# Row normalisation moved to GpSimd, separate slots for the shared passes, and a first q projection in two column groups, in a fused attention and gated MLP kernel

## The chip, the cores and the metric

The kernel runs on one core of a Trainium2 chip. The core has five engines that run side by side, each through its own queue in order: TensorE (PE, matrix products into PSUM; its weight loads are listed as PEld), VectorE (DVE), ScalarE (ACT), GpSimd (POOL) and SyncE (SP, which issues the DMAs). They wait for each other through semaphores. The metric is the device time of one execution in microseconds.

## The reference

The input x has 2048 rows of 512. It is normalised by rows, and two branches read the result: an attention with 32 heads of 16 columns, and a gated MLP with 1792 hidden columns. Their sum is added to x.

```python
S, D, H, F = 2048, 512, 32, 1792
xn = (x - mean(x)) / sqrt(var(x) + 1e-5)                  # by rows
q, k, v = split((xn @ wqkv).reshape(S, 3, H, 16))
p = softmax(q @ k.T * 16 ** -0.5)                          # per head, 2048 x 2048
attn = (p @ v).reshape(S, D) @ wo
gate, up = xn @ W_gate, xn @ W_up
mlp = (gate * (gate > 0) * up) @ W_down
out = x + attn + mlp                                       # bf16
```

## The kernel before

**Units and quads.** The scores are made transposed, keys on the partitions and 512 query columns (a block `c4`, four of them) along the free dimension. Heads are worked in groups: `gg` (four groups of eight heads) and `ee` (the even or the odd heads of a group). For one key tile `kt` of 128 keys there are four heads. In most cases ScalarE takes the exponential of two of them at a time, one instruction on 128 x 1024 elements (line 1392): this is a *unit*, and there are 720. For the rest of the key tiles a *quad* does it without ScalarE: VectorE brings each of four score tiles out of PSUM into 16-bit integers (line 1345, four instructions), and two copies of the 2048 columns, shifted by a constant, are made: one by GpSimd (line 1361, two pieces), the other in six quads of ten by GpSimd too and else by VectorE (line 1365); VectorE makes both in the last two quads. The integers are read as bf16 bit patterns, so that three patterns together stand for the exponential. `QUADS` says how many quads a block of sixteen key tiles has (mostly five), `LAST_QUADS` stretches their places in the last block, and `SC_ORDER` is the order of the four heads of a quad on TensorE.

**TensorE.** A product with 64 rows of weights occupies one half of the array, `half` 0 or 1; the halves work at the same time. Heads 0 and 1 of a quad lie on half 0, heads 2 and 3 on half 1. Scores, the products with V (line 1297 loads their weights), the gate, up and down projections, the projections of q, k and v, and the output rows all go through line 124 or 849, in half-array passes of four instructions each. Background work (projections, MLP, output rows) is spread between the units by a list of slots.

**PSUM.** Banks 0, 1, 4 and 5 are two double buffers for units (`P_sc`); banks 6, 7, 2 and 3 are the pool `P_b` for everything else.

**The order.** The kernel records operations with dependencies and estimated durations (`G.op`). A planner (`Graph.run`) then walks through them by estimated time and writes the order of each engine's queue; `prio` ranks what is ready, `after` holds an operation until a unit has gone by, and `order` is an order without a wait. Operations with `port=True` on VectorE and GpSimd are planned so that they don't overlap, and such an operation of GpSimd waits for the VectorE one before it. The order is fixed when the program is built; on the chip each queue is strictly in order.

**The start.** `ln_block(b, pr)` normalises block `b`: VectorE takes the statistics of four row tiles (line 767, then 768), GpSimd the reciprocal root (line 762, with the variance plus epsilon of line 760), and a VectorE pass subtracts and scales (line 780, `xn_sb`). Blocks 0 and 1 are transposed by TensorE (line 803) and brought back by ScalarE (block 0, line 811) or VectorE (block 1, line 819); blocks 2 and 3 are transposed by DMAs (`DMA_TR`). Then `proj_q(0, 0)` projects the first q (line 842) and masks it for four heads into `qT`: masks 0 and 2 on ScalarE (line 886), masks 1 and 3 later on VectorE (line 887). The first K tile is projected in two pieces (line 966) and brought out by VectorE (line 970). Later K goes through line 907 and V through line 914 (`v_aug`); `V_AT` says from which unit on the V tiles of each block are asked for. TensorE runs products of zeros in gaps of the start (lines 953 and 1407).

**The end.** The last block's output rows are closed by `normalise_last`: the last sums of the products with V are brought out, turned into reciprocals and multiplied, and the last output projection follows (lines 1158 to 1189).

Of the kernel before, what the change touches and what calls it, by code (L numbers as in the profile page):

```python
# [10 lines left out]
ACTF = mybir.ActivationFunctionType  # L11
ALU = mybir.AluOpType
# [15 lines left out]
BANK = (6, 7, 2, 3)  # L28
# [4 lines left out]
PV_SLACK = 50  # L33
W_STEP = 6
D_STEP = 3
W_LEAD = 34
Q_LEAD = 40
K_LEAD = 32
QN, KN, GN, RN = 2, 2, 5, 10
# [20 lines left out]
REC_SLACK = 3000  # L60
SP_SLACK = 2000
TAIL_URGENT = 3
RB_KB = 33
RBZ_AT = 20
SC_ORDER = (0, 1, 2, 3)
P1_OFF = 0
LAST_QUADS = 0.9
SPLIT = 8
PVBANKS = (0, 1, 2, 3)
PV_EARLY = False  # L70
# [14 lines left out]
Z_AT = 10  # L85
MASK_ACT = (0, 2)
MASK_LATE = 4
PER_TILE = (0, 1)
V_AT = (4, 10, 18, 26)
EXP_SCALE = 1.0 / (128.0 * LOG2E)  # L90
NUP = 1
NHS = 20
# [36 lines left out]
class Graph:  # L129
# [6 lines left out]
    ISSUE = 16.0  # L136
    FILL = 425.0
    NEAR = 20
    DMA_SLACK = 1000
    FILL_MIN = 230.0  # L140
    AHEAD_LOADS = 4
# [55 lines left out]
    def run(self):  # L197
# [16 lines left out]
        n = 0  # L214
# [33 lines left out]
        def ready(o):  # L248
            at = 0.0
            for d in o.deps:  # L250
                at = max(at, d.end if d.eng == "PE" else d.end + ((0.0 if d.urgent else max(self.DMA_SLACK, o.slack)) if d.eng == "SP" else o.slack))
            for d in o.order:
                at = max(at, d.start if d.eng == o.eng else d.end)
            for t in o.acq:
                if t.slot is not None:
                    continue
                b = slot_for(t)
                if b is None:
                    return None
                at = max(at, b[0] + (o.slack if o.eng == "SP" else 0.0))  # L260
            return at
# [46 lines left out]
        port = {"DVE": (0.0, None), "POOL": (0.0, None)}  # L308
# [19 lines left out]
        while n < len(ops):  # L328
# [247 lines left out]
def bass_parallel_sum__mha_block__glu_gated_reglu__prompt_kernel(  # L576
# [14 lines left out]
    with ExitStack() as es:  # L591
# [25 lines left out]
        kT = sb("kT", [128, NGG, S], BF16)  # L617
# [52 lines left out]
             reads=[t_id], writes=[t_id], prio=-898)  # L670
        t_rbz = Tile()
        for i in range(2):
            G.op("POOL", 460, lambda e, i=i: e.memset(rb[:, i, :], 1.0), writes=[Tile()], prio=RBZ_AT, after=RBZ_AT)
            t_rbz.w.append(G.ops[-1])
        t_vones, t_woz, t_selp, t_shift = Tile(), Tile(), Tile(), Tile()
        for i in range(2):
# [15 lines left out]
        def xs(m):  # L692
            return x_sb[:, m, :] if m < 8 else hT[:, m - 8, :]
# [54 lines left out]
                t_wol.w.append(G.ops[-1])  # L748

        t_xnT = [Tile() for _ in range(NB)]  # L750

        def ln_block(b, pr):

            first, single = b == 0, b in PER_TILE
            t_rs = [Tile() for _ in range(4)]
            t_mvs = Tile()

            def inv(m, n, rd, wr):
                t_ve = Tile()
                G.op("DVE" if single else "POOL", 66 if single else 230, lambda e: e.tensor_scalar(vare[:, m:m + n], mv[:, m:m + n, 1], EPS, None, op0=ALU.add),  # L760
                     reads=[rd], writes=[t_ve], prio=pr)
                G.op("POOL", 400 + 160 * n, lambda e: e.tensor_tensor(rstd[:, m:m + n], vare[:, m:m + n], expo[:, 0:n], ALU.pow),
                     reads=[t_ve, t_expo], writes=[wr], prio=pr)
            for i in range(4):
                m = 4 * b + i
                t_st, t_mv = Tile(), Tile()
                G.op("DVE", 580, lambda e, m=m: e.bn_stats(stats[:, m, :], xs(m)), reads=[t_xm[m]], writes=[t_st], prio=pr)  # L767
                G.op("DVE", 90, lambda e, m=m: e.bn_aggr(mv[:, m, :], stats[:, m, :]), reads=[t_st], writes=[t_mv], prio=pr - 0.1)
                t_mvs.w.append(G.ops[-1])
                if single:  # L770
                    inv(m, 1, t_mv, t_rs[i])
            if not single:
                inv(4 * b, 4, t_mvs, t_rs[0])
                t_rs = [t_rs[0]] * 4
            if first:
                tp0, tp1 = Tile("tp0", P_sc, [0]), Tile("tp1", P_sc, [1])
            for i in range(4):
                m = 4 * b + i
                t_n = Tile("xn", P_xn)
                G.op("DVE", 320, lambda e, m=m, t=t_n: e.tensor_scalar(  # L780
                    xn_sb[:, t.slot, :], xs(m), mv[:, m, 0:1], rstd[:, m:m + 1], op0=ALU.subtract, op1=ALU.mult),
                    reads=[t_xm[m], t_rs[i]], writes=[t_n], prio=pr + 0.2)
# [12 lines left out]

                def bank(tp=tp, i=i):
                    return (ps[:, 4 * (i // 2) + i % 2, :] if first else ps[:, BANK[tp.slot], :]).bitcast(BF16)

                def tr(e, t=t_n, bank=bank, half=half):
                    ins = None  # L800
                    for dt in range(DT):
                        c0 = 512 * half + 128 * dt
                        ins = e.transpose(bank()[:, c0:c0 + 128], xn_sb[:, t.slot, 128 * dt:128 * dt + 128], ident[:])  # L803
                    return ins
                o = G.op("PE", 450, tr, reads=[t_n, t_id], writes=[tp], prio=pr, name="tr", urgent=TR_URGENT[b], after=TR_AFTER[b])
                if first:
                    o.deps = {w: True for w in o.deps if w.eng != "ACT"}
                if first:
                    def ev(e, bank=bank, m=m):
                        src = bank()[:, 0:512].rearrange("p (dt c) -> p dt c", dt=DT)  # L810
                        return e.activation(xnT[:, :, 128 * m:128 * m + 128], src, ACTF.Copy)
                    o = G.op("ACT", 560, ev, reads=[tp], writes=[Tile()], prio=pr + 0.1)
                    o.deps = {w: True for w in o.deps if w is tp.w[-1]}
                    t_xnT[b].w.append(o)
                elif half == 1:
                    def ev(e, bank=bank, m=m):
                        src = bank().rearrange("p (m dt c) -> p m dt c", m=2, dt=DT)
                        dst = xnT[:, :, 128 * m - 128:128 * m + 128].rearrange("p dt (m c) -> p m dt c", m=2)
# [141 lines left out]
        for bank, c, tk in ((1, slice(0, 128), t_k0), (2, slice(128, 512), t_k[(0, 0)])):  # L960
            t = Tile("prok", P_b, [bank])
            for dt in range(DT):
                def kfirst(e, bank=bank, c=c, dt=dt):
                    ins = None
                    for j in range(4):
                        ins = e.matmul(ps[32 * j:32 * j + 32, BANK[bank], c], Wk[:, dt, 32 * j:32 * j + 32], xnT[:, dt, c],  # L966
                                       start=(dt == 0), stop=(dt == DT - 1), tile_position=(0, 32 * j))
                    return ins
                G.op("PE", (c.stop - c.start) * 0.42, kfirst, reads=[t_wk[0], t_xnT[0]], writes=[t], prio=-789 + 0.1 * bank, mode="col")
            G.op("DVE", 70 + (c.stop - c.start) * 1.04, lambda e, bank=bank, c=c: e.tensor_copy(kT[:, 0, c], ps[:, BANK[bank], c]), reads=[t], writes=[tk],  # L970
                 prio=-795 + bank)

        def key_tiles(gg, kt):
            return t_k0 if gg == kt == 0 else t_k[(gg, kt // 4)]
# [470 lines left out]
```

## Time and profile before

| | us |
|---|---|
| median of the three runs (694.37 to 698.17) | 697.02 |
| the profiled execution | 694.96 |
| its span | 693.1 |
| ScalarE busy | 669.3 |
| TensorE busy (matrix products) | 678.2 |
| VectorE busy | 596.1 |
| GpSimd busy | 534.0 |

Times in a timeline count from the start of the span. A timeline row gives the start, the time until the last of the merged instructions ended, the engine, the line, the operation, its output and inputs, how many instructions are merged, and in square brackets the idle time before it with what ended it. A row of the groups gives the busy time, the mean duration of one in ns, and the idle time of the engine ahead of the group. Instructions overlap in their pipelines, so the mean duration is longer than the distance from one start to the next, and a busy TensorE isn't one at its full rate. The granted TensorE clock is 1.00 from the start to 680 us.

### The profile page before, as it was taken

What the parts mean: (1) busy time and instruction counts of PE and PEld (TensorE: products, weight loads), DVE (VectorE), ACT (ScalarE), POOL (GpSimd) and SP (SyncE); (2) the same over time, 40 slices, a digit from 0 to 9 for tenths busy, and PEclk for the clock granted to TensorE, in tenths of its full rate; (3) what the DMA queues carried; (4) which work ended last, traced back from release to release, by engine and by line L of the source; (5) the groups of instructions that cost most, each with busy time, mean ns of one, the idle gap of its engine ahead of it and who ended that gap; (6) DMA issues with size and microseconds to landing.
All of it is one profiled execution on the core that took longest, in us unless ns stands there. A gap on an engine that the chain in (4) does not pass through costs nothing.

```text
span 693.1 us, 46178 instructions
## 1 busy us (share of the span) xinstructions
PE 678.2 (98%) x22215; PEld 380.5 (55%) x20739; DVE 596.1 (86%) x992; ACT 669.3 (97%) x731; POOL 534.0 (77%) x543
## 2 busy tenths in 40 slices
PE   8999999999999999999999999999999999999996
PEld 3445555555654656565554556655554455666553
DVE  8957999988899788999998788999899687899775
ACT  5999999999999999999999999999999998999994
POOL 3422678787898898897988888798798985878880
PEclk9999999999999999999999999999999999999999
DMA  7231111232201112111101112011100121111001
GB/s 213 52 62 34 32 32 42 46 103 74 77 23 29 43 51 55 27 48 29 30 13 38 35 41 71 20 48 20 46 12 18 42 74 46 50 49 34 22 19 38
DMA packets 55820, 31.87 MB, mean 46 GB/s; under 512 B 21196, under 2 KB 53644, under 8 KB 55628
## 3 DMA queue, kind: packets, MB, share of 16 engines
q1 hardware_dynamic: 55628, 28.92, 16.2%
q8 instruction: 168, 2.75, 1.7%
q14 instruction: 24, 0.20, 0.1%
HBM read 22.28 MB, written 2.35 MB: 36 GB/s over the span
## 4 chain that ended last, share of the span: by engine, by line
PE 63%; ACT 30%; DVE 5%; issue 1%; DMA 0%; DVEq 0%; POOL 0%
PE ps L124 62%; ACT ring L1392 30%; DVE qd L1345 2%; DVE xn_sb L780 1%; DVE stats L767 1%; DVE v_aug L914 1%; DMA x_sb<-in_A_x_dram 0%; DVE qT L887 0%; DVE qd L1365 0%; PE ps L1143 0%; PE ps L842 0%; PE ps L1407 0%; PE ps L803 0%; DVEq L554 0%; PE ps L966 0%
## 5 line engine op out<-in xcount | busy, mean ns | idle before, releaser
L1392 ACT ACTIVATE ring<-ps 128x1024 bf16<-128x1024 f32 x720 | 662.9, 1109 | 6.6 <-PE ps L124 6.2
L1361 POOL TENSOR_TENSOR qd<-qd,ints 128x512 int32<-128x512 int32 x480 | 483.5, 1041 | 120.0 <-DVE qd L1345 57.0
L124 PE MATMUL ps<-qT,kT 64*32 64x512 bf16 x8192 | 461.3, 375 | 3.3 <-ACT ring L1392 1.1
L1345 DVE TENSOR_SCALAR qd<-ps 128x512 int16<-128x512 f32 x608 | 396.4, 684 | 61.0 <-PE ps L124 56.6
L124 PE MATMUL ps<-qd,v_aug 64*32 64x512 bf16 x3648 | 289.6, 375 | 0.3
L124 PE MATMUL ps<-ring,v_aug 64*32 64x512 bf16 x2880 | 250.7, 375 | 2.0 <-DVE v_aug L914 1.7
L1325 PEld LDWEIGHTS <-kT 64*32 64x32 bf16 x7916 | 167.9, 92 | 121.8 <-issue 32.4
L1297 PEld LDWEIGHTS <-v_aug 64*32 64x32 bf16 x5328 | 128.7, 92 | 76.8 <-issue 17.6
L124 PE MATMUL ps<-xnT,wgs 64*32 64x512 bf16 x1792 | 138.1, 375 | 0.2
L124 PE MATMUL ps<-xnT,wus 64*32 64x512 bf16 x1792 | 136.7, 375 | 0.0
L124 PE MATMUL ps<-Wd,hT 64*32 64x512 bf16 x768 | 57.6, 375 | 0.6 <-DVE rrec L1235 0.6
L849 PEld LDWEIGHTS <-wgs 64*32 64x32 bf16 x1792 | 43.8, 92 | 24.8 <-issue 5.1
L849 PEld LDWEIGHTS <-hT 64*32 64x32 bf16 x1792 | 42.2, 92 | 24.9 <-issue 2.6
L849 PEld LDWEIGHTS <-wus 64*32 64x32 bf16 x1792 | 43.5, 92 | 20.7 <-issue 3.1
L1365 DVE TENSOR_SCALAR qd<-qd 128x2048 int16<-128x2048 int16 x64 | 51.8, 821 | 1.7 <-PE ps L124 1.0
L1021 DVE COPY up_sb<-ps 128x512 f32<-128x512 f32 x56 | 38.3, 683 | 4.6 <-PE ps L124 4.0
L1025 DVE SCALAR_TENSOR_TENSOR hT<-ps,up_sb 128x512 bf16<-128x512 f32 x56 | 38.0, 679 | 3.0 <-PE ps L124 2.8
L124 PE MATMUL ps<-Wv,hT 64*32 64x512 bf16 x512 | 39.9, 376 | 0.0
L124 PE MATMUL ps<-Wk,hT 64*32 64x512 bf16 x512 | 39.4, 375 | 0.0
L124 PE MATMUL ps<-xnT,Wq 64*32 64x512 bf16 x480 | 37.3, 375 | 0.4 <-issue 0.3
L124 PE MATMUL ps<-xnT,Wk 64*32 64x512 bf16 x480 | 37.0, 375 | 0.0
L124 PE MATMUL ps<-Wo_p,x_sb 64*32 64x512 bf16 x480 | 36.4, 376 | 0.3 <-issue 0.3
(72 smaller groups left out, 264.0 us busy)
## 6 DMA issues: line engine op xcount, KB each, us to landing
wus<-in_B_W_up_dram SPq DMA_DIRECT2D x38, 128.0 KB, 2.6
wgs<-in_B_W_gate_dram SPq DMA_DIRECT2D x38, 128.0 KB, 2.8
rb<-rec_scr SPq DMA_DIRECT2D x124, 32.0 KB, 2.8
xr_sb<-in_A_x_dram SPq DMA_DIRECT2D x16, 128.0 KB, 2.6
out_dram<-xn_sb SPq DMA_DIRECT2D x16, 128.0 KB, 1.8
qT<-qf SPq DMA_DIRECT2D x120, 16.0 KB, 2.2
x_sb<-in_A_x_dram SPq DMA_DIRECT2D x8, 128.0 KB, 2.8
x_sb<-oT SPq DMA_DIRECT2D x60, 16.0 KB, 2.4
```

The source lines that it names most:

```text
L124: return e.add_instruction(mybir.InstMatmult(name=e.bass.get_next_instruction_name(), engine=mybir.EngineType.PE, ins=[e.lower_ap(x), e.lo ...
L767: G.op("DVE", 580, lambda e, m=m: e.bn_stats(stats[:, m, :], xs(m)), reads=[t_xm[m]], writes=[t_st], prio=pr)
L780: G.op("DVE", 320, lambda e, m=m, t=t_n: e.tensor_scalar(xn_sb[:, t.slot, :], xs(m), mv[:, m, 0:1], rstd[:, m:m + 1], op0=ALU.subtract, op ...
L849: e.ldweights(w()[rows, 32 * j:32 * j + 32], tile_position=(rows.start, 32 * j))
L1021: G.op("DVE", 603, lambda e: e.tensor_copy(up_sb[:, tup.slot, :], bank_of(tu)), reads=[tu], writes=[tup], prio=-590)
L1025: G.op("DVE", 603, lambda e: e.scalar_tensor_tensor(out=hT[:, th.slot, :], in0=bank_of(tg), scalar=0.0, in1=up_sb[:, tup.slot, :], op0=ALU ...
L1297: e.ldweights(vs(j), tile_position=(64 * half, 32 * j))
L1325: e.ldweights(ks(m), tile_position=(64 * half, 32 * m))
L1345: G.op("DVE", 601, lambda e, j=j, tx=tx: e.tensor_scalar(qd[:, tq.slot, 512 * j:512 * j + 512], ps[:, BANK[tx.slot], :], IBIAS[3], 0.0, op ...
L1361: G.op("POOL", POOL_NS / POOL_PIECES + 60, lambda e, x=x, n=n, c=slice(i * m, i * m + m): e.tensor_tensor(x().bitcast(I32)[:, c], raw().bi ...
L1365: G.op("DVE", 600, lambda e, n=n, x=x: e.tensor_scalar(x(), raw(), float(SHIFTS[n + 1]), None, op0=ALU.add), reads=[ti, tq], writes=[t], p ...
L1392: exp_ops[u] = G.op("ACT", 904, lambda e, tr=tr, k0=k0: e.activation(ring[:, tr.slot, :, :], ps[:, 4 * k0:4 * k0 + 2, :], ACTF.Exp, scale= ...
```

## The change

It has these parts:

- The passes that normalise the rows of blocks 2 and 3 (eight instructions) are issued on GpSimd, with an estimate of 900 ns.
- More operations are marked `port=True`: these eight, VectorE's four passes of block 1, and GpSimd's fills of `rb` and `qT`.
- The planner's estimate between two dependent VectorE operations falls by 90 ns (`OWN`).
- The statistics of block 1 are ordered behind the last pass of block 0.
- The first q projection is made in two column groups, 384 columns as soon as three row tiles are transposed and 128 columns behind the fourth; the masks are made in the same two pieces. The projection of the first 128 keys stands before it, that of the other 384 behind it.
- Constants: `SC_ORDER`, `LAST_QUADS`, `V_AT` and `W_LEAD` (how many units ahead the MLP's weights are asked for).

Since the planner works through all of it, the queues of TensorE and VectorE are in another order over the whole kernel.

```diff
-W_LEAD = 34
+W_LEAD = 32
...
+XN_POOL = (2, 3)
+XN_NS = 900
...
-SC_ORDER = (0, 1, 2, 3)
+SC_ORDER = (0, 2, 1, 3)
...
-LAST_QUADS = 0.9
+LAST_QUADS = 0.95
...
-V_AT = (4, 10, 18, 26)
+V_AT = (4, 8, 24, 32)
...
+    OWN = 90.0
...
-                at = max(at, d.end if d.eng == "PE" else d.end + ((0.0 if d.urgent else max(self.DMA_SLACK, o.slack)) if d.eng == "SP" else o.slack))
+                at = max(at, d.end - (self.OWN if d.eng == o.eng == "DVE" else 0.0) if d.eng == "PE" or d.eng == o.eng == "DVE" else d.end + ((0.0 if d.urgent else max(self.DMA_SLACK, o.slack)) if d.eng == "SP" else o.slack))
...
-            G.op("POOL", 460, lambda e, i=i: e.memset(rb[:, i, :], 1.0), writes=[Tile()], prio=RBZ_AT, after=RBZ_AT)
+            G.op("POOL", 460, lambda e, i=i: e.memset(rb[:, i, :], 1.0), writes=[Tile()], prio=RBZ_AT, after=RBZ_AT, port=True)
...
+        last_xn = []
...
-                G.op("DVE", 580, lambda e, m=m: e.bn_stats(stats[:, m, :], xs(m)), reads=[t_xm[m]], writes=[t_st], prio=pr)
+                G.op("DVE", 580, lambda e, m=m: e.bn_stats(stats[:, m, :], xs(m)), reads=[t_xm[m]], writes=[t_st], prio=pr, order=last_xn if m == 4 else ())
...
-                G.op("DVE", 320, lambda e, m=m, t=t_n: e.tensor_scalar(
+                G.op("POOL" if b in XN_POOL else "DVE", XN_NS if b in XN_POOL else 320, lambda e, m=m, t=t_n: e.tensor_scalar(
                     xn_sb[:, t.slot, :], xs(m), mv[:, m, 0:1], rstd[:, m:m + 1], op0=ALU.subtract, op1=ALU.mult),
-                    reads=[t_xm[m], t_rs[i]], writes=[t_n], prio=pr + 0.2)
+                    reads=[t_xm[m], t_rs[i]], writes=[t_n], prio=pr + 0.2, port=b > 0)
                 t_x[b].r.append(G.ops[-1])
+                if first:
+                    last_xn[:] = G.ops[-1:]
...
-            G.op("POOL", 460, lambda e, i=i: e.memset(qT[:, 1, i, :], 0.0), writes=[Tile()], prio=Z_AT, after=Z_AT)
+            G.op("POOL", 460, lambda e, i=i: e.memset(qT[:, 1, i, :], 0.0), writes=[Tile()], prio=Z_AT, after=Z_AT, port=True)
...
-        proj_q(0, 0, -790, tile=pb, sub=0, eng="ACT")
+        upto = [Tile() for _ in range(4)]
+        for i in range(4):
+            upto[i].w = t_xnT[0].w[:i + 1]
...
+        def first(tile, w, t_w, bank, c, x, need, prio):
             for dt in range(DT):
...
+                o = G.op("PE", (c.stop - c.start) * 0.42, mm, reads=[t_w, upto[need]], writes=[tile] if dt == 0 else [], prio=prio, mode="col")
...
+        first(bk, Wk, t_wk[0], 1, slice(0, 128), slice(0, 128), 0, -789.5)
+        G.op("DVE", 200, lambda e: e.tensor_copy(kT[:, 0, 0:128], ps[:, BANK[1], 0:128]), reads=[bk], writes=[t_k0], prio=-795, order=last_xn)
...
+        first(pb, Wq, t_wq[0], 3, slice(0, 384), slice(0, 384), 2, -789)
+        first(bq, Wq, t_wq[0], 1, slice(128, 256), slice(384, 512), 3, -788)
...
+        for v in (0, 2, 1, 3):
...
+            for n, (tile, bank, c, x) in enumerate(((pb, 3, slice(0, 384), slice(0, 384)), (bq, 1, slice(128, 256), slice(384, 512)))):
+                late = v not in (0, 2) and not n
+                G.op("ACT" if act else "DVE", (150 if act else 100) + (0.92 if act else 1.04) * (x.stop - x.start),
...
+        kr = Tile("prok", P_b, [2])
+        first(kr, Wk, t_wk[0], 2, slice(128, 512), slice(128, 512), 3, -786)
+        G.op("DVE", 470, lambda e: e.tensor_copy(kT[:, 0, 128:512], ps[:, BANK[2], 128:512]), reads=[kr], writes=[t_k[(0, 0)]], prio=-793)
```

More of the change, by code (lines that the diff above doesn't have):

```diff
@@ L957, in bass_parallel_sum__mha_block__glu_gated_reglu__prompt_kernel @@
         pb = Tile("pro", P_b, [3])
-        proj_q(0, 0, -790, tile=pb, sub=0, eng="ACT")
+        q0 = q_slot[(0, 0)] = Tile("q", P_q)
+        upto = [Tile() for _ in range(4)]
+        for i in range(4):
+            upto[i].w = t_xnT[0].w[:i + 1]
         t_k0, t_k[(0, 0)] = Tile("k"), Tile("k")
-        for bank, c, tk in ((1, slice(0, 128), t_k0), (2, slice(128, 512), t_k[(0, 0)])):
-            t = Tile("prok", P_b, [bank])
+        bk = Tile("prok", P_b, [1])
+        def first(tile, w, t_w, bank, c, x, need, prio):
@@ L962, in bass_parallel_sum__mha_block__glu_gated_reglu__prompt_kernel, with mm @@
             for dt in range(DT):
-                def kfirst(e, bank=bank, c=c, dt=dt):
+                def mm(e, dt=dt):
                     ins = None
                     for j in range(4):
-                        ins = e.matmul(ps[32 * j:32 * j + 32, BANK[bank], c], Wk[:, dt, 32 * j:32 * j + 32], xnT[:, dt, c],
+                        ins = e.matmul(ps[32 * j:32 * j + 32, BANK[bank], c], w[:, dt, 32 * j:32 * j + 32], xnT[:, dt, x],
                                        start=(dt == 0), stop=(dt == DT - 1), tile_position=(0, 32 * j))
@@ L968, in kfirst @@
                     return ins
-                G.op("PE", (c.stop - c.start) * 0.42, kfirst, reads=[t_wk[0], t_xnT[0]], writes=[t], prio=-789 + 0.1 * bank, mode="col")
-            G.op("DVE", 70 + (c.stop - c.start) * 1.04, lambda e, bank=bank, c=c: e.tensor_copy(kT[:, 0, c], ps[:, BANK[bank], c]), reads=[t], writes=[tk],
-                 prio=-795 + bank)
+                o = G.op("PE", (c.stop - c.start) * 0.42, mm, reads=[t_w, upto[need]], writes=[tile] if dt == 0 else [], prio=prio, mode="col")
@@ new lines, in first @@
+                if dt:
+                    tile.w.append(o)
+            return o
+        first(bk, Wk, t_wk[0], 1, slice(0, 128), slice(0, 128), 0, -789.5)
+        G.op("DVE", 200, lambda e: e.tensor_copy(kT[:, 0, 0:128], ps[:, BANK[1], 0:128]), reads=[bk], writes=[t_k0], prio=-795, order=last_xn)
+        bq = Tile()
+        bq.w, bq.r = list(bk.w), list(bk.r)
+        k0 = len(G.ops)
+        first(pb, Wq, t_wq[0], 3, slice(0, 384), slice(0, 384), 2, -789)
+        first(bq, Wq, t_wq[0], 1, slice(128, 256), slice(384, 512), 3, -788)
@@ new lines, in bass_parallel_sum__mha_block__glu_gated_reglu__prompt_kernel @@
+        bk.r += [o for o in G.ops[k0:] if o in bq.w]
+        on_act = []
+        for v in (0, 2, 1, 3):
+            t1 = Tile("q%d" % v)
+            t_q.setdefault((0, 0, v % 2), []).append(t1)
+            act = v in MASK_ACT
+            for n, (tile, bank, c, x) in enumerate(((pb, 3, slice(0, 384), slice(0, 384)), (bq, 1, slice(128, 256), slice(384, 512)))):
+                late = v not in (0, 2) and not n
+                G.op("ACT" if act else "DVE", (150 if act else 100) + (0.92 if act else 1.04) * (x.stop - x.start),
+                     (lambda e, v=v, bank=bank, c=c, x=x: e.activation(qT[:, q0.slot, v, x], ps[:, BANK[bank], c], ACTF.Copy, scale=hmask[:, v:v + 1]))
+                     if act else (lambda e, v=v, bank=bank, c=c, x=x: e.tensor_scalar(qT[:, q0.slot, v, x], ps[:, BANK[bank], c], hmask[:, v:v + 1], None, op0=ALU.mult)),
+                     reads=[tile, t_masks[v]], writes=[] if n else [t1], joins=[q0], prio=MASK_LATE + v if late else -787 + 0.2 * v + 0.1 * n,
+                     after=MASK_LATE + v if late else None)
+                if n:
+                    t1.w.append(G.ops[-1])
+                    if not act:
+                        for w in on_act:
+                            G.ops[-1].deps[w] = True
+                    else:
+                        on_act.append(G.ops[-1])
+                    bk.r.append(G.ops[-1])
```

## The prediction

> **What bounds the kernel now.** I read the head of the page first, for the busy shares and for the chain that ended last.
>
> ```profile
> span 693.1 us, 46178 instructions
> PE 678.2 (98%) x22215; PEld 380.5 (55%) x20739; DVE 596.1 (86%) x992; ACT 669.3 (97%) x731; POOL 534.0 (77%) x543
> PE 63%; ACT 30%; DVE 5%; issue 1%; DMA 0%; DVEq 0%; POOL 0%
> L1392 ACT ACTIVATE ring<-ps 128x1024 bf16<-128x1024 f32 x720 | 662.9, 1109 | 6.6 <-PE ps L124 6.2
> ```
>
> ScalarE and TensorE are both full, and the chain changes between them. ScalarE's 720 exponentials are the fixed work. From the trace's start times, the median distance between two of them is 0.904 us, the first starts at 12.47 and the last at 680.33. 719 distances of 0.904 are 650.0, so 667.9 - 650.0 = 17.9 us are lost between the first and the last; 12.5 lie ahead of the first and 12.8 behind the start of the last. No edit changes the count of exponentials, so these three amounts are all there is to win.
>
> Next, ScalarE's timeline, where each row is a run of exponentials without a visible pause.
>
> ```profile
> 10.69 1.27 ACT L886 ACTIVATE qT<-ps,hmask 128x512 bf16<-128x512 f32 x2 [1.24 <-PE ps L842]
> 12.47 15.69 ACT L1392 ACTIVATE ring<-ps 128x1024 bf16<-128x1024 f32 x17 [0.52 <-PE ps L124]
> 29.04 8.36 ACT L1392 ACTIVATE ring<-ps 128x1024 bf16<-128x1024 f32 x9 [0.87 <-PE ps L124]
> 38.17 9.43 ACT L1392 ACTIVATE ring<-ps 128x1024 bf16<-128x1024 f32 x10 [0.79 <-PE ps L124]
> 48.44 39.62 ACT L1392 ACTIVATE ring<-ps 128x1024 bf16<-128x1024 f32 x43 [0.83 <-PE ps L124]
> 583.37 3.77 ACT L1392 ACTIVATE ring<-ps 128x1024 bf16<-128x1024 f32 x4 [0.98 <-PE ps L124]
> ```
>
> Three stops of about 0.8 us fall in the first 50 us; by start distances they cost 1.07, 0.99 and 0.95, together 3.0 us. One more knot stands at 577 to 587 us. Why the early ones arise is in the timelines of TensorE and VectorE:
>
> ```profile
> 27.91 0.39 PE L124 MATMUL ps<-ring,v_aug 64*32 64x512 bf16 x4 [1.15 <-DVE v_aug L914]
> 37.05 0.39 PE L124 MATMUL ps<-ring,v_aug 64*32 64x512 bf16 x4 [0.59 <-DVE v_aug L914]
> 23.82 2.18 DVE L780 TENSOR_SCALAR xn_sb<-hT,mv,rstd 128x512 bf16<-128x512 bf16 x2
> 34.60 1.80 DVE L780 TENSOR_SCALAR xn_sb<-hT,mv,rstd 128x512 bf16<-128x512 bf16 x2
> 23.67 2.18 POOL L1361 TENSOR_TENSOR qd<-qd,ints 128x512 int32<-128x512 int32 x2 [3.37 <-DVE qd L1345]
> ```
>
> TensorE stands before a product that needs a V copy (L914), and in VectorE's queue those copies stand behind the row passes of blocks 2 and 3 (L780). Such a pass takes 0.41 us when GpSimd is idle; beside GpSimd's L1361 two of them take 2.18. From 17 to 37 us VectorE has no pause.
>
> **The start.** The first exponential now waits for one q projection of 512 columns (L842, 9.59, sixteen products in 0.86 us until L966 starts at 10.45), both masks (1.27), and a TensorE queue that does all of K and two transposes first (scores at 12.01). In the new order the first row block's fourth pass comes no earlier: the statistics of block 1 no longer stand before it (L767, 7.36, 0.69), but its 1/sqrt on GpSimd is also asked for later. By the rows that ends at 7.13 (variance) + 0.2 + 0.57 = 7.9, against 7.96 before. What is won lies behind it. The transpose ends at 8.82, q of 384 columns takes 0.65 and its result is there at 9.75, 0.9 before L886 starts now. The four mask pieces on ScalarE: 1024 columns cost 0.904, 512 about 0.59, so 0.61 ns a column and 0.28 fixed; 384 then cost 0.51 and 128 cost 0.36. Mask 0 ends at 10.7, mask 2 at 11.45; the first scores need mask 0 alone and are ready at 11.2. First exponential at 11.45: **-1.0 us** (between -0.6 and -1.3).
>
> Part of it is given back. VectorE now waits from 7.2 to 7.9, with block 1's statistics behind that, so block 1's passes run about 1.1 us later (the last at 13.4 instead of 12.35). The TensorE queue holds three transposes of block 1 before the fourth unit's scores: 13.4 + 0.41 + 0.25, scores at 14.2, exponential at 14.65, where 11.45 + 3 x 0.904 = 14.16 was due: **+0.5** (0 to +1.0). Queued behind that wait are all of TensorE's scores; the other two masks, moved to VectorE in pieces, cost 0.4 more in the same queue, inside this range.
>
> **Eight row passes go to GpSimd.** On VectorE the eight take 0.35 + 2.42 + 0.65 + 1.72 = 5.14 us from start to start. GpSimd shows no such instruction; the nearest rows are a fill of 512 columns (L681, 0.52, nothing read) and a product of two float inputs (L1252, 1.28); a cast of 128 columns (L678, 0.29) scaled by columns gives about 0.9, and with one tensor input that is the row it is nearest to. Block 2's reciprocal root, at 18.1 now and up to 1.5 later in the new order, plus 4 x 0.9 ends by 23.3 (21.8 to 24.8), ahead of VectorE's 26.0 today, so its transposes on SyncE and K of block 2 come no later; in GpSimd's own queue the q fills (1.92) and the first L1361 stand behind. Up to 1.58 us a pass nothing is late. With 5.1 us less on VectorE the V copies come off the queue, and V of blocks 2 and 3 is asked for six units later. Of the 3.0 us I take **-2.2** (-3.0 to 0; zero if the copies stay late).
>
> **Order everywhere else.** Quads now score heads 0, 2, 1, 3, so neighbours lie on different halves of the array; the planner's VectorE latency falls by 90 ns; GpSimd's fills and passes are planned apart from VectorE's. Costs in instructions: none but 75 more groups of four weight loads, 0.1 us each (L1325's 92 ns, overlapped), in PEld's 45% of idle time; uncovered they would cost 7.5 us. The order shows: of the 719 distances between unit scores, 174 hold five or more half-array passes on the fuller half before, 149 after; one of nine and one of seven, at units 35 and 37 (the stop at 47.6), are gone; a half that follows itself in the queue falls from 554 runs to 497. By the trace's start distances within one half, a pass takes 0.2165, so 4.18 fit in 0.904. Against it, stretches of 20 units that need 4.2 were one and are four. I take **-1.0** of the remaining loss, bounds -3 and +5. Weight loads asked for two units later (W_LEAD) cost nothing: 32 units are 29 us, and they land in 2.6 to 2.8; late by more than 26 us they would stop the gate and up products.
>
> **The end.** The last quad moves one key tile later. Behind the last score stand 8 passes on the fuller half before, 12 after: 4 x 0.2165 = **+0.9** (0 if TensorE runs ahead).
>
> **Sum.** -1.0 + 0.5 - 2.2 - 1.0 + 0.9 = -2.8. The profiled execution took 694.96 (693.1 and 1.86 around), so 692.2 on its scale; the median of the runs shown is 2.06 higher, which would be 694.2. The runs scatter by 3.8, so I put the forecast between: **693.0**. Half a per cent (3.5 us) is about what a measurement of this kernel can tell from no change.
>
> **Rivals.** First, *the gain moves along*: the fourth unit loses 1.0, the V copies keep half their stops (VectorE still has no pause until 30 us), the end pays 0.9, and the order gives nothing: -1.0 + 1.0 - 1.5 + 0.9 = -0.6, time 696. For it: the TensorE queue is written by estimates, and each stop removed leaves the next due within 0.3 us. Against: 5.1 us of VectorE work really goes.
>
> Second, *a new knot*, slower: the stretches at 4.2 half passes have no slack, so an eviction that is late stops ScalarE, as at 577 to 587 us, where 20 units lost 2.57 against the usual 0.25 and four evictions (L1345) stand in a row. Three such knots more cost 7.0 and the order's -1.0 is lost: -2.8 + 1.0 + 7.0 = +5.2, time 702. The kernel is slower than before from the second knot on (+2.8), and by over half a per cent from the third. For it: four stretches over 4.18. Against: no window of two units needs ten passes any longer (six before).
>
> Third, *the port turned round*: GpSimd's passes hold what VectorE's need. Two passes cost 2.18 beside L1361 instead of 0.7; if four of VectorE's remaining passes meet a 0.9 us pass, VectorE gets 3.6 of its 5.1 us back, the -2.2 shrinks to -0.5, and the time is 695 to 697. [...] Against it here: the order puts VectorE's PSUM copies beside GpSimd's first four passes.
>
> **Chances.** Forecast 0.47 (its own range 688 to 693.5), gain moves along 0.28, port 0.06, new knot 0.19. The forecast case is the faster one; the second and third are within half a per cent; the knot is slower. The range takes in the rivals up to one knot and the lower bounds of the start and order terms: 687.5 to 700.5.
>
> **What would show it.** First exponential at 11.3 to 11.6; fourth at 14.2 to 14.8; no stop over 0.5 us on ScalarE from 25 to 50; GpSimd's passes at 0.7 to 1.1; VectorE's first pause before 33; from the last exponential's start to the end 12.8 to 13.7. Wrong would be a first exponential at 12 or later, passes over 1.6, or over 15 us lost between exponentials behind unit 60.

## Result and the profile after

The changed kernel took 704.52 us (median of four runs, 702.98 to 705.00) beside 696.35 for the kernel before: a ratio of 1.0114, 95% interval 1.0081 to 1.0147. It is slower by 1.1%, where 693.0 was forecast; the time lies above the whole range (687.5 to 700.5). The profiled execution took 704.2, with a span of 702.3.

The head of the page, the chain, and the costliest group:

```profile
span 702.3 us, 46519 instructions
PE 680.4 (97%) x22230; PEld 382.7 (54%) x21056; DVE 592.6 (84%) x986; ACT 671.4 (96%) x733; POOL 550.4 (78%) x551
PE 60%; ACT 30%; POOL 4%; DVE 4%; issue 1%; DMA 0%; DVEq 0%; POOLq 0%
L1438 ACT ACTIVATE ring<-ps 128x1024 bf16<-128x1024 f32 x720 | 664.9, 1109 | 14.3 <-PE ps L126 13.7
```

ScalarE's idle time before an exponential (last column) has more than doubled, from 6.6 to 14.3, and GpSimd stands with 4% in the chain in which it had none. One exponential costs the same (1109 ns). ScalarE's timeline shows the place:

```profile
11.18 1.96 ACT L1438 ACTIVATE ring<-ps 128x1024 bf16<-128x1024 f32 x2
13.51 1.02 ACT L1438 ACTIVATE ring<-ps 128x1024 bf16<-128x1024 f32 x1 [0.37 <-PE ps L126]
14.99 26.86 ACT L1438 ACTIVATE ring<-ps 128x1024 bf16<-128x1024 f32 x29 [0.46 <-PE ps L126]
49.44 1.02 ACT L1438 ACTIVATE ring<-ps 128x1024 bf16<-128x1024 f32 x1 [7.58 <-PE ps L126]
51.15 1.02 ACT L1438 ACTIVATE ring<-ps 128x1024 bf16<-128x1024 f32 x1 [0.68 <-PE ps L126]
52.64 8.37 ACT L1438 ACTIVATE ring<-ps 128x1024 bf16<-128x1024 f32 x9 [0.47 <-PE ps L126]
```

The first exponential is 1.29 earlier than before, and the early stops (29.04 and 38.17 in the kernel before) are gone. In their place stands one stop of 7.58, with two smaller ones behind it. TensorE's timeline says what it waited for, and GpSimd's when that came:

```profile
45.61 0.59 PE L126 MATMUL ps<-qd,v_aug 64*32 64x512 bf16 x4 [4.94 <-POOL qd L1407]
47.73 0.58 PE L126 MATMUL ps<-qd,v_aug 64*32 64x512 bf16 x4 [1.53 <-POOL qd L1407]
```

```profile
20.22 8.25 POOL L784 TENSOR_SCALAR xn_sb<-hT,mv,rstd 128x512 bf16<-128x512 bf16 x4
34.14 8.25 POOL L784 TENSOR_SCALAR xn_sb<-hT,mv,rstd 128x512 bf16<-128x512 bf16 x4
43.28 1.04 POOL L1407 TENSOR_TENSOR qd<-qd,ints 128x512 int32<-128x512 int32 x1
44.52 1.04 POOL L1407 TENSOR_TENSOR qd<-qd,ints 128x512 int32<-128x512 int32 x1
45.65 2.04 POOL L1407 TENSOR_TENSOR qd<-qd,ints 128x512 int32<-128x512 int32 x2
```

Four row passes take 8.25 us, 2.06 each from start to start. The copies of a quad (L1407, two pieces for each copy) stand behind the second four and two fills; TensorE asked for them at 40.67 (45.61 less the 4.94 of idle time) and could go on at 45.61. The windows of one us (PE, PEld, DVE, ACT, POOL busy and, in the column behind POOL, the granted TensorE clock) show what followed the idle time:

```profile
44.00:45.00 1.00, 0.00 (x0) 0.00 (x0) 0.00 (x0) 0.00 (x0) 1.00 (x3) 1.00 0.30 63
45.00:46.00 1.00, 0.39 (x8) 0.10 (x4) 0.00 (x0) 0.00 (x0) 1.00 (x3) 0.71 0.75 208
51.00:52.00 1.00, 1.00 (x32) 0.71 (x20) 0.00 (x0) 0.85 (x1) 0.00 (x0) 0.50 0.06 16
52.00:53.00 1.00, 1.00 (x44) 0.93 (x36) 0.25 (x1) 0.53 (x2) 0.00 (x0) 0.87 0.00 0
```

The clock falls to half at about 45.4 and is back at about 52.3, so the work that had piled up ran at half speed: two groups of K products in a row start 0.43 apart (51.10 and 51.53), behind 52.3 they start 0.22 apart (52.32 and 52.54), and a group takes 0.58 to 0.67 in place of 0.38.

The difference of the spans, 9.2 us, splits by the starts of the exponentials (each stretch less 0.904 a distance):

| | before | after | difference |
|---|---|---|---|
| start of the first | 12.47 | 11.18 | -1.3 |
| lost in the first 20 distances | 1.2 | 1.4 | +0.2 |
| distances 20 to 40 | 2.2 | 9.5 | +7.2 |
| distances 40 to 60 | 0.3 | 0.4 | +0.1 |
| behind 60 | 14.1 | 17.0 | +2.8 |
| from the last start to the end | 12.8 | 12.9 | +0.2 |

### The profile page after: what moved, and what is told of

Same layout as the page of the kernel before. It is cut to its first block, busy times and chain, and to the rows that moved or that the text cites. A ratio compares the mean times of both kernels' runs of the same rounds, so it can differ in the third digit from the quotient of the medians.

```text
span 702.3 us, 46519 instructions
## 1 busy us (share of the span) xinstructions
PE 680.4 (97%) x22230; PEld 382.7 (54%) x21056; DVE 592.6 (84%) x986; ACT 671.4 (96%) x733; POOL 550.4 (78%) x551
## 4 chain that ended last, share of the span: by engine, by line
PE 60%; ACT 30%; POOL 4%; DVE 4%; issue 1%; DMA 0%; DVEq 0%; POOLq 0%
PE ps L126 59%; ACT ring L1438 30%; POOL xn_sb L784 2%; DVE qd L1391 1%; DVE stats L771 1%; POOL qd L1407 1%; POOL rstd L766 0%; DVE xn_sb L784 0%; DMA x_sb<-in_A_x_dram 0%; DVE qd L1411 0%; POOL qT L834 0%; DVE mv L772 0%; DVE xnT L825 0%; PE ps L1189 0%; DVE qT L1003 0%
## 5 line engine op out<-in xcount | busy, mean ns | idle before, releaser
L1438 ACT ACTIVATE ring<-ps 128x1024 bf16<-128x1024 f32 x720 | 664.9, 1109 | 14.3 <-PE ps L126 13.7
L1407 POOL TENSOR_TENSOR qd<-qd,ints 128x512 int32<-128x512 int32 x480 | 483.7, 1039 | 114.7 <-DVE qd L1411 51.3
L1391 DVE TENSOR_SCALAR qd<-ps 128x512 int16<-128x512 f32 x608 | 398.6, 683 | 64.2 <-PE ps L126 57.5
L126 PE MATMUL ps<-qd,v_aug 64*32 64x512 bf16 x3648 | 297.2, 376 | 7.7 <-POOL qd L1407 6.5
L1371 PEld LDWEIGHTS <-kT 64*32 64x32 bf16 x8136 | 172.9, 92 | 121.6 <-issue 27.4
L1343 PEld LDWEIGHTS <-v_aug 64*32 64x32 bf16 x5408 | 131.8, 92 | 72.1 <-issue 16.3
```

What stands on the lines that cost most here:

```text
L126: return e.add_instruction(mybir.InstMatmult(name=e.bass.get_next_instruction_name(), engine=mybir.EngineType.PE, ins=[e.lower_ap(x), e.lo ...
L1343: e.ldweights(vs(j), tile_position=(64 * half, 32 * j))
L1371: e.ldweights(ks(m), tile_position=(64 * half, 32 * m))
L1391: G.op("DVE", 601, lambda e, j=j, tx=tx: e.tensor_scalar(qd[:, tq.slot, 512 * j:512 * j + 512], ps[:, BANK[tx.slot], :], IBIAS[3], 0.0, op ...
L1407: G.op("POOL", POOL_NS / POOL_PIECES + 60, lambda e, x=x, n=n, c=slice(i * m, i * m + m): e.tensor_tensor(x().bitcast(I32)[:, c], raw().bi ...
L1438: exp_ops[u] = G.op("ACT", 904, lambda e, tr=tr, k0=k0: e.activation(ring[:, tr.slot, :, :], ps[:, 4 * k0:4 * k0 + 2, :], ACTF.Exp, scale= ...
```

## Experiments

Ratios are to the kernel before, measured beside it on the same chip; "lost in 20 to 40" is as in the table.

**The row passes back on VectorE.**

```diff
-XN_POOL = (2, 3)
+XN_POOL = ()
```

> The changed kernel with its eight row passes of blocks 2 and 3 on VectorE again (XN_POOL empty), all else kept. Theory A, the GpSimd pass: one takes 2.08 us where the planner had 0.9, so the first quads' patterns come late in GpSimd's queue, TensorE stands 4.9 and 1.5 us before them from 40.7 us on, and works on at half the clock until 52.5; without it no stop over 1.5 us is left in the first 60 us, and the time falls from 704.5 to 694 to 698, with the first exponential still at 11.2. Rival B, the order: the reordered quads, the port marks and the new start cost the time by themselves, and it stays at 700 or over.

Measured: 1.0007 (0.9996 to 1.0018). The first exponential starts at 11.05, and 3.3 us are lost in 20 to 40. In a later measurement, the same kernel: 0.9999 (0.9983 to 1.0016). All the rest of the change together is worth nothing that can be measured; the loss belongs to the passes on GpSimd and to the order that was written for them. One stop over 1.5 us is left, which theory A did not expect, and it is of another kind:

```profile
48.22 12.02 ACT L1438 ACTIVATE ring<-ps 128x1024 bf16<-128x1024 f32 x13 [2.82 <-PE ps L126]
```

TensorE is busy all the way to it and its clock stays at 1.00; the queue has 15 passes on the fuller half, mostly K and V of the last block, between two units' scores.

The stops at 29.04 and 38.17 of the kernel before stay away here too, although the passes are on VectorE. Four of them stand in a row:

```profile
33.29 1.38 DVE L784 TENSOR_SCALAR xn_sb<-hT,mv,rstd 128x512 bf16<-128x512 bf16 x4
```

Each takes 0.41, none lies beside a copy of GpSimd (which waits for them at 34.75), and all eight take 2.6 us from start to start, where the kernel before needed 5.14. So about half of the VectorE time that the move was to win is there without the move. The new order keeps the two engines apart; which part of the change does that was not tried alone.

**A true estimate for the planner.**

```diff
-XN_NS = 900
+XN_NS = 2080
```

> The changed kernel with the planner told what a GpSimd row pass takes (XN_NS 2080 instead of 900), the passes still on GpSimd. Theory A1, the estimate: TensorE's queue then holds other work while GpSimd is busy, the stop of 7.9 us at the 32nd exponential is gone or under 2 us, and the time is 694 to 698. Rival A2, GpSimd is too slow whatever the order: K and V of blocks 2 and 3 and the first quads' patterns come 8 us later than on VectorE and ScalarE loses at least 4 us in the first 60 us, time 700 or over.

Measured: 1.0046 (1.0029 to 1.0062). TensorE no longer waits for the quad's copies, so some 0.7% is regained, but 6.2 us are lost in 20 to 40: the K products of the late blocks now come together, 17 passes on the fuller half between two units' scores, and for the last 0.58 us TensorE waits for a K copy of VectorE. The largest stop stands behind that:

```profile
51.19 9.31 ACT L1438 ACTIVATE ring<-ps 128x1024 bf16<-128x1024 f32 x10 [4.76 <-PE ps L126]
```

Each theory has one sign for it: the time is theory A1's, the stop is rival A2's. With passes as slow as they are, the order written for 900 ns thus costs some 0.7%. The 0.5% that is left is again a matter of order; what a slow pass costs by itself is not shown.

**The passes alone, on the kernel before.**

```diff
-                G.op("DVE", 320, ...
+                G.op("POOL" if b in (2, 3) else "DVE", 900 if b in (2, 3) else 320, ...
```

> The kernel before with one part of the change alone: the eight row passes of blocks 2 and 3 on GpSimd, estimate 0.9 us, marked for the shared port. Theory A: the stop comes here too, 5 to 9 us in the first 60 us, time 701 to 705 against 696 to 697. Rival B: 698 or less, since the pass alone isn't the trouble.

Measured: 1.0048 (1.0030 to 1.0066), between the two theories. The stop at 29.04 is gone (0.1 us lost in the first 20 distances, 1.2 before), but 5.2 us are lost in 20 to 40. Here TensorE waits for the transposes of block 3's rows:

```profile
43.90 0.38 PE L124 MATMUL ps<-xnT,Wk 64*32 64x512 bf16 x4 [2.44 <-DMA xnT<-xn_sb]
```

The late pass hurts in either order, but which wait ends last is different: in this one K of block 3, in the changed kernel a quad's copies.

**GpSimd's forms, one beside the other** (in the kernel before, on a buffer that isn't yet in use):

```diff
+            lambda e: e.tensor_scalar(o16, i16, h0, h1, op0=ALU.subtract, op1=ALU.mult),
+            lambda e: e.tensor_scalar(o16[:, 0:256], i16[:, 0:256], h0, h1, op0=ALU.subtract, op1=ALU.mult),
+            lambda e: e.tensor_scalar(o16, i16, h0, None, op0=ALU.mult),
+            lambda e: e.tensor_scalar(o16, i16, 0.5, 2.0, op0=ALU.subtract, op1=ALU.mult),
+            lambda e: e.tensor_scalar(scf, i16, h0, h1, op0=ALU.subtract, op1=ALU.mult),
+            lambda e: e.tensor_copy(o16, i16),
+            lambda e: e.tensor_tensor(o16, i16, h0.to_broadcast([128, 512]), ALU.subtract),
```

> The kernel before, with seven extra GpSimd instructions on a scratch tile in GpSimd's idle time near 40 to 60 us; the output is not touched. They are the row pass in seven forms: (1) two pointer scalars, bf16, 512 columns; (2) the same, 256 columns; (3) one pointer scalar; (4) two constants; (5) two pointer scalars with a float32 output; (6) a plain copy; (7) a subtraction of a broadcast column as a two-input operation. If the two pointer scalars make the pass slow, (1) and (2) show about 4 ns a column and (4) and (6) under 2; if any one-input bf16 operation is that slow on GpSimd, all are near 2 us; if it is a fixed cost, (2) is over 1.5 us.

Measured, in GpSimd's timeline (start, duration):

```profile
40.23 2.09 POOL L690 TENSOR_SCALAR Wo_p<-Wo_p,hmask 128x512 bf16<-128x512 bf16 x1
42.42 1.22 POOL L691 TENSOR_SCALAR Wo_p<-Wo_p,hmask 128x256 bf16<-128x256 bf16 x1
43.74 1.57 POOL L692 TENSOR_SCALAR Wo_p<-Wo_p,hmask 128x512 bf16<-128x512 bf16 x1
45.40 1.94 POOL L693 TENSOR_SCALAR Wo_p<-Wo_p 128x512 bf16<-128x512 bf16 x1
47.44 2.08 POOL L694 TENSOR_SCALAR Wo_p<-Wo_p,hmask 128x512 f32<-128x512 bf16 x1
49.58 0.61 POOL L695 COPY Wo_p<-Wo_p 128x512 bf16<-128x512 bf16 x1
50.27 1.04 POOL L696 TENSOR_TENSOR Wo_p<-Wo_p,hmask 128x512 bf16<-128x512 bf16 x1
```

With a tensor and two scalars it takes 2.09 whether the scalars are columns or constants (1.94) and whether bf16 or float is written (2.08); half the columns take 1.22, so (2.09 - 1.22) / 256 = 3.4 ns a column and 0.35 fixed. One operation takes 1.57, a copy 0.61, a subtraction of a broadcast column 1.04. In these forms the slowness goes with the instruction, not with its operands.

**Shorter passes in the same order.** Since the estimate stays at 900, every queue keeps the changed kernel's order; the pass alone is shorter. It leaves out the subtraction of the mean for blocks 2 and 3, so the output is not the reference's, and the kernel serves for the time alone.

```diff
-                ... e.tensor_scalar(
-                    xn_sb[:, t.slot, :], xs(m), mv[:, m, 0:1], rstd[:, m:m + 1], op0=ALU.subtract, op1=ALU.mult),
+                ... e.tensor_tensor(
+                    xn_sb[:, t.slot, :], xs(m), rstd[:, m:m + 1].to_broadcast([128, D]), ALU.mult)
```

> The changed kernel with every queue in the same order, but GpSimd's eight row passes are one multiplication by the broadcast reciprocal root (1.04 us in the run of forms) in place of the subtract and multiply (2.08); the subtraction of the mean is left out for the rows of blocks 2 and 3. Theory A, the duration of the pass is the whole cause: the first exponential stays at 11.1 to 11.2, the stop at unit 31 (7.85) and the slow clock behind it (1.4) go, the first 40 units lose 1.3 to 3.0 in place of 10.8, the later units lose as much as in the changed kernel (about 16), and the time is 8 to 9.5 us under the changed kernel's: 0.995 to 1.000 of the kernel before. Theory B, the new order is bad by itself (the p3 piece behind the passes, the shared port, the transposes by DMA): the stop at 40 us stays over 3 us and the ratio over 1.004. Theory C, my forecast with the right duration: the forecast's order term (-1.0) was right as well, ratio 0.994 to 0.996.

Measured: 0.9989 (0.9963 to 1.0015); 1.1 us lost in 20 to 40. GpSimd's and ScalarE's timelines:

```profile
30.22 4.04 POOL L784 TENSOR_TENSOR xn_sb<-hT,rstd 128x512 bf16<-128x512 bf16 x4
36.38 1.04 POOL L1408 TENSOR_TENSOR qd<-qd,ints 128x512 int32<-128x512 int32 x1
37.50 2.04 POOL L1408 TENSOR_TENSOR qd<-qd,ints 128x512 int32<-128x512 int32 x2
```

```profile
14.93 32.47 ACT L1439 ACTIVATE ring<-ps 128x1024 bf16<-128x1024 f32 x35 [0.46 <-PE ps L126]
47.73 13.10 ACT L1439 ACTIVATE ring<-ps 128x1024 bf16<-128x1024 f32 x14 [0.34 <-PE ps L126]
```

The copies are there at 37.4 and 39.5, before TensorE asks, and the stop is gone with nothing changed but the duration of the pass: theory A. The order by itself is not at fault; it fails with a pass that takes longer than it was written for. Even so no gain is left to be measured (theory C, 0.994 to 0.996, lies just outside the interval).

**Passes of a length between** (the mean is left out here too).

```diff
-                    xn_sb[:, t.slot, :], xs(m), mv[:, m, 0:1], rstd[:, m:m + 1], op0=ALU.subtract, op1=ALU.mult),
+                    xn_sb[:, t.slot, :], xs(m), rstd[:, m:m + 1], None, op0=ALU.mult)
```

> The changed kernel with every queue in the same order, the eight GpSimd passes as one multiplication by a column (1.57 us in the run of forms, between 1.04 and 2.08); the subtraction of the mean is left out for the rows of blocks 2 and 3. Theory A, a due point: with passes of 1.04 the second quad's GpSimd pieces ended at 37.4, with 2.08 at 45.6, and TensorE asked for them at 40.7. Eight times 0.53 more than 1.04 puts them at 41.6: 0.9 late, the next pair at 43.8, 1.5 late, of which ScalarE sees some 1 to 2.5 us; ratio 1.000 to 1.003 of the kernel before. Theory B, the loss grows in proportion to the pass (8.3 us for 1.04 us a pass more): 4.2 us at 1.57, ratio 1.004 to 1.006. My forecast's own point (nothing late up to 1.58 us) says no stop over 0.5 us between 30 and 50 us, ratio 0.998 to 1.000.

Measured: 1.0075 (1.0047 to 1.0102); 4.7 us lost in 20 to 40. GpSimd, TensorE and two windows:

```profile
40.81 1.04 POOL L1408 TENSOR_TENSOR qd<-qd,ints 128x512 int32<-128x512 int32 x1
41.94 2.04 POOL L1408 TENSOR_TENSOR qd<-qd,ints 128x512 int32<-128x512 int32 x2
```

```profile
41.90 0.38 PE L126 MATMUL ps<-qd,v_aug 64*32 64x512 bf16 x4 [0.70 <-POOL qd L1408]
44.03 0.59 PE L126 MATMUL ps<-qd,v_aug 64*32 64x512 bf16 x4 [1.74 <-POOL qd L1408]
```

```profile
43.00:44.00 1.00, 0.00 (x0) 0.00 (x0) 0.00 (x0) 0.00 (x0) 1.00 (x2) 0.84 0.37 106
47.00:48.00 1.00, 1.00 (x44) 0.83 (x32) 0.00 (x0) 0.64 (x1) 0.00 (x0) 0.95 0.19 48
```

The due point is as worked out: the copies end at 41.85 and 43.98 (expected 41.6 and 43.8), and TensorE stands for 0.70 and 1.74. The price was put too low: behind 2.4 us of waiting the clock was at 0.50 from 43.7 to 47.1, and ScalarE lost 4.4 at this place in place of 1 to 2.5, which is as much as theory B said. The two theories are told apart by the waits and not by the time: 1.0075 lies above both ranges, and its interval takes in part of theory B's. The limit of this order can be worked out from the kernel with passes of 1.04, in which TensorE came to the products of the second quad without a wait. The one that needs the second pair of copies is this:

```profile
40.66 0.38 PE L126 MATMUL ps<-qd,v_aug 64*32 64x512 bf16 x4
```

The pair had ended at 39.54, so eight passes could each be (40.66 - 39.54) / 8 = 0.14 longer, about 1.2 us. The first pair leaves more room: 37.42, taken up at 40.44.

**The start alone, on the kernel before** (the two-column first q projection and the order of block 1's statistics; no port marks, no 90 ns, constants and row passes as before).

> The kernel before with the two-column first q projection and the order of block 1's statistics alone: no port marks, no 90 ns, constants and row passes as before. Theory A: first exponential 11.0 to 11.2 (-1.3 to -1.4), +1.0 given back at the second to fourth exponential, and the planner puts 23 half-array passes ahead of unit 36's scores (before: 9): 23 x 0.2165 - 0.904 = 4.1 lost there in place of 0.95, so the ratio is 1.003 to 1.006. Rival: TensorE runs ahead of the exponentials and hides most of the 23 passes, so the gain of the start stays: ratio 0.997 to 1.000.

Measured: 1.0066 (1.0038 to 1.0093), a little above theory A's range; the first exponential starts at 11.06, and 8.0 us are lost in the first 40 distances, 4.4 of them at unit 36, where theory A had 4.1: the planner puts 23 half-array passes ahead of its scores. The 1.4 us won at the start are lost several times over.

**The constants alone, on the kernel before.**

```diff
-W_LEAD = 34
+W_LEAD = 32
-SC_ORDER = (0, 1, 2, 3)
+SC_ORDER = (0, 2, 1, 3)
-LAST_QUADS = 0.9
+LAST_QUADS = 0.95
-V_AT = (4, 10, 18, 26)
+V_AT = (4, 8, 24, 32)
```

> The kernel before with the four constants alone (score order 0, 2, 1, 3, last quads 0.95, V at 4, 8, 24, 32, weights' lead 32). First exponential as before, 12.47; knots of 9 and 7 passes at units 35 and 37, as before. Theory A (the constants only move knots): ratio 0.998 to 1.002, lost behind the last exponential's start 12.8 to 13.2. My forecast's order term (-1.0 of the remaining loss) would be a ratio of 0.997 to 0.9985. Rival, V at 24 and 32 bunches V and K of the last block: over 1.002.

Measured: 1.0041 (1.0026 to 1.0055), worse than theory A said. The ratio is the rival's, but not for its reason, V and K bunched: 2.1 us are lost in 20 to 40, where before it was 2.2. The loss is at the end, where 15.8 us pass from the last exponential's start, in place of 12.8; ScalarE waits 3.55 for the last sums, before 0.47. Which of the four constants does it was not tried.

**The constants of before, all else as changed and row passes on VectorE.**

```diff
+XN_POOL = ()
+V_AT = (4, 10, 18, 26)
+SC_ORDER = (0, 1, 2, 3)
+LAST_QUADS = 0.9
+W_LEAD = 34
```

> The changed kernel with the row passes on VectorE and the four constants (score order of the quads, places of the last quads, V times, lead of the MLP's weights) of the kernel before: what is left is the two-column start, the port marks and the 90 ns. The count of half-array passes between unit scores has 9, 6, 7 and 6 at units 27, 29, 35 and 37, where the version with vector rows has 15 and 7 at 35 and 37. Theory A, a stop is that count: 15 passes are 3.25 us against 0.90, and 3.08 us were lost there; here the backlog is 1.4 in place of 2.6, so units 20 to 40 lose about 2.2 in place of 3.28, the start is the same (11.05), behind the last score stand 30 passes in place of 19 (up to +2.4 at the end): ratio 0.997 to 1.002. Theory B, the constants carry a gain spread over the later units: the units behind 60 lose more than in the version with vector rows (11.5), and the ratio is 1.002 or more.

Measured: 0.9965 (0.9933 to 0.9998). It looked like a version that beats both, so it was measured again beside the version with vector rows and the changed constants:

> The version with row passes on VectorE and the constants of the kernel before, which had 0.9965 with an interval that almost touches 1, in more rounds and beside the version with the changed constants on one chip. Theory A (the start gives 1.4, of which about 1.1 comes back at the second to fourth exponential, and port marks and 90 ns take the knots out of 27 to 40): 0.995 to 0.999. Rival, chance of one chip: 0.999 to 1.001.

> The version with row passes on VectorE and all else as changed, beside the one above. It has 15 half-array passes ahead of unit 36's scores, and 3.1 us were lost there, where the version above loses about 1. Theory A: 2 us slower than the version above by that stop, the rest equal: ratio 0.998 to 1.001, as 1.0007 before. Rival, the constants are worth something elsewhere: within 0.5 us of the version above.

Measured: 0.9993 (0.9977 to 1.0008) with the constants of before and 0.9999 (0.9983 to 1.0016) with the changed ones. No gain over the kernel before is shown. The stop of 3.1 us is there with the changed constants and not with those of before (3.4 and 1.7 lost in 20 to 40), but the end takes most of it back: 13.3 from the last start to the end against 14.4, and the two spans are 689.9 and 690.0.

**Other times for V.** Row passes on VectorE, score order of before, V of the last blocks asked for at units 16 and 24.

> A candidate for the fastest: two-column start, port marks and 90 ns, row passes on VectorE, score order of the kernel before, V of blocks 2 and 3 asked for at units 16 and 24. Counts between unit scores 9, 6, 7, 7 at units 27 to 37 (backlog 1.4), 20 passes behind the last score as in the kernel before. By theory A (the count tells the stop): first exponential 11.05, units 20 to 40 lose 2.0 to 2.5, end as before: -1.4 + 1.2 + 0 = 0.996 to 0.9995 of the kernel before. By the rival that four stretches of 20 units over 4.18 passes (one before) cost 1 to 2 us, 1.000 to 1.002.

Measured: 0.9969 (0.9942 to 0.9995), beside the 0.9965 above, which the later measurement didn't bear out; this version was not measured a second time, so a gain is not shown. Lost in 20 to 40: 1.9, a little under what the count said.

## Why the prediction was wrong

**The step that failed is "Eight row passes go to GpSimd".** It put a pass at 0.9 us, by scaling a cast of 128 columns, between 0.52 and 1.28. (Four times the cast's 0.29 would be 1.16; the step doesn't say what it took off.) Measured are 2.08, outside both bounds: the rows taken as ends were a fill, which reads nothing, and a product of two tensors, and neither is an instruction with two scalars. The cast was no neighbour either; a copy of 512 columns is quick (0.61), one operation makes it 1.57 and two 2.09. The step's own point, "up to 1.58 us a pass nothing is late", is wrong too, though by less: the limit of this order is about 1.2. It was worked out for block 2, whose passes delay only their transposes. What came late was behind block 3's passes: the copies of the second quad in GpSimd's own queue. The prediction named the first L1361 as standing behind and gave it no due time.

So the term was not -2.2 but about +6: the two V-copy stops did go (they had cost 1.07 and 0.99), as forecast, but distances 20 to 40, the second of these stops included, lost 7.2 us more than before; less the 1.07 of the first stop that makes +6.1.

The rest of the step holds up. With passes of 1.04 and the same queues, the three early stops (3.0 us) shrink to one of 0.48, so -2.5 where -2.2 was forecast. But the move was not needed for the two V-copy stops: with the passes on VectorE and the rest as changed, they are gone as well.

**TensorE's queue is fixed.** The planner wrote it for passes of 900 ns. A product of the quad stood ahead of scores and projections that needed nothing from GpSimd, and all of them waited. The prediction had rival cases for stops by tight stretches of TensorE, not for a single late input. Its second rival gave 702 (counted from 697.02; from the 695.8 that the forecast starts from it is 701), not far from what was measured, but by three more knots put down to late evictions of VectorE. Here one input of GpSimd was late, so that the number is near is luck. The prediction's sign of being wrong "passes over 1.6" was the right one to look at, and no chance had been given to it. The other sign, over 15 us lost behind unit 60, came too (17.0), but it can't be told from the scatter below.

**The start** was right in its mechanism: 11.18 where 11.45 was forecast. The give-back was larger, 1.1 at the second and third distances (0.52 and 0.58) against +0.5: K of 384 columns comes out of PSUM at 12.09, behind block 1's statistics, and TensorE stands 0.42 us for it at 12.70, ahead of the third unit's scores; the transposes then delay the fourth, which starts at 14.99 (14.65 forecast).

**VectorE** came off its queue as said: its first pause of over a microsecond begins at 32.4, with nothing like it from 17 to 37 us before. The **port** rival showed next to nothing. VectorE's remaining row passes were done at 14.1, and GpSimd's begin at 20.22. Two statistics of VectorE beside GpSimd's passes (20.26) took 1.27, and 1.25 without them (15.93). Two copies out of PSUM beside GpSimd's passes (L1391, 21.45 and 22.77) took 0.67 and 0.68, where the mean of the 608 is 0.68. One instruction was longer beside a pass of GpSimd, by some 0.4 us; the same one takes 0.68 where GpSimd is idle (39 of its 64 times):

```profile
26.64 1.06 DVE L1411 TENSOR_SCALAR qd<-qd 128x2048 int16<-128x2048 int16 x1
```

**The order everywhere else** (-1.0) is not borne out. With the same order in three kernels, single executions lost 13.7, 17.0 and 19.3 behind distance 60 (before: 14.1), so an effect of 1 us can't be read from one profile; by the ratios, all of the change without the passes is worth 1.0007 and 0.9999. **The end** cost 0.2 and not 0.9.

**Parts do not add.** Start alone 1.0066, constants alone 1.0041, passes alone 1.0048: together with the port marks and the 90 ns, but without the passes, 1.000. Each part makes the planner write another order. The start alone loses at the projections ahead of unit 36, the passes alone at K of block 3, the constants alone at the end, a few us each time. The port marks and the 90 ns were not tried alone.

## What to carry to other kernels

Before work is moved to another engine, find a row of that very instruction form there, or measure it in a spare place of the kernel; a row of another form need not bound it (here 0.52 and 1.28 stood on both sides of the estimate, and the pass took 2.08). Then go down that engine's queue behind the moved work and give each thing that another engine waits for its due time: the first one that is late sets the price. Where a queue's order is written from estimates, a wrong estimate can cost more than the work that was moved (here 7.2 us lost in 20 to 40 for 5.1 us taken off VectorE), since everything behind the wait stands too.

## What was unexpected of the hardware

GpSimd's TENSOR_SCALAR on 128x512 bf16 takes 2.09 us with two operations and 1.57 with one; a copy takes 0.61. The two-operation pass that took VectorE 0.41 alone takes GpSimd five times as long.

The granted clock fell to 0.50 behind 4.94 us of idle TensorE (45.4 to 52.3), behind 2.44 in the kernel with the passes alone (44.4 to 47.8), and behind waits of 0.70 and 1.74 with a few products between them (43.7 to 47.1); it stayed at 1.00 in the stops in which TensorE was busy with projections (46 to 48 in the kernel with vector rows, 47 to 50 with the true estimate). The slow stretch is 3.4 us or twice that (6.8). In two of the cases TensorE had not been idle for all of the 3.4 us before the fall: in the last one it was at work for about 1.3 of them, by the one-us windows (all of 40.28 to 41.0, then 0.29 and 0.29), and with the passes alone for 0.97 (41.02 to 41.46 and 43.90 to 44.43).
